# Value matmuls in four column tiles of 32, another order of the first pair, and half of the input weights decoded from round 18 on

## The chip, the cores and the metric

The kernel runs on one core of a Trainium2 chip. The core has a matrix engine (TensorE, PE in the rows; its weight loads are PEld), a vector engine (VectorE, DVE), a scalar engine (ScalarE, ACT), GpSimd (POOL) and SyncE (SP), which issues most DMAs. Each engine runs its own list of instructions in order and waits on semaphores for the others. The metric is device time in microseconds, the median of several runs.

## What is computed

Three layers, one after the other, for 2 batches, 12 heads, 448 positions, head size 64:

```python
# attention with a soft cap
scores = cap * tanh(q @ k.T / sqrt(64) / cap)
attn = exp(scores - max) ; attn = attn / (sum(attn) + 1e-9)
x = attn @ v                                  # heads side by side: 448 x 768
# gated MLP with a spatial gate
u, v = split(gelu(x @ w_in))                  # w_in 768 x 1024
x = x + (u * (w_sg @ layernorm(v) + b_sg)) @ w_out
# gated MLP with a convolution of 3 positions
h = relu(x @ w2_in)                           # 768 x 1024
out = (h * sigmoid(conv(h))) @ w2_out         # 1024 x 768
```

## The kernel before

Attention comes first, in 12 pairs of heads (N), each in two halves; a half is a round R = 2N + half, and two more rounds follow. All matmuls of attention go through `ordered`, which pins each behind the one before it, so TensorE's order is the order of the code. A round has these parts:

- `scores(N, half)` (line 308) writes keys times queries into the tile `sc`, four banks, one buffer. Keys stand in four blocks g of 128. For g = 0 to 2 each head has its own matmuls, on its half of the partitions, two at a time; g = 3 holds the last 64 keys of one head and the first 64 of the other in one matmul. Half 0 has g = 0 and 1 (12 matmuls), half 1 has g = 2 and 3 (9). ScalarE then does tanh (line 317, out of `sc` into `raw`) and exp (line 318, in `raw`). For pair 0 tanh and exp go block by block. The next scores need the banks that tanh has read.
- `values(N, half)` (line 344) runs a round later, from round 13 on two. It multiplies `raw` with the values into the tile `pv` (lines 353 to 361: two matmuls of 64 columns for each g below 3, one of 128 columns for g = 3, in float32, each of which the profile shows as two instructions), and then sums `raw` over the keys into `su` (lines 363 to 372) in four column tiles of 32, on half 0 by way of `sm`, in which VectorE has added two blocks (line 342). `su` has one buffer, which VectorE copies into `se` (line 389); ScalarE copies `pv` into `E` (line 390).
- `norm` sends the sums through DMAs (`ss`, `d`, `rb`), VectorE multiplies and splits into `X`. The last pair goes through TensorE instead (`norm_pe`, line 431, tiles `r` and `rp`; `rp` lies in the bank of `su`).
- `prep_q` and `prep_k` split a later pair's queries and keys on VectorE.
- A piece of the input weights w_in (12 pieces of 128 rows and 512 columns, 0 to 5 into `WI0`, 6 to 11 into `WI1`) is loaded by SP in the round that the table `WIN` names, `int(at * 4 + 1) // 2`, and decoded from 64-bit words some ticks later (`decode`, line 121; two ticks a round): ScalarE line 130, VectorE lines 135, 140, 143, 149 and 152, tile `f`. Before: rounds 0, 2, 4, 5, 7, 9, 11, 13, 14, 16, 18, 20.
- In the rounds of the table `FILL` (13, 17, 21: 6 matmuls; 23, 25: 18 matmuls) TensorE also does parts of x @ w_in with `WI0` (tile `mo`).

Ahead of it all, `WARM` matmuls of zeros run while the first loads are under way, and `IDLE` matmuls of zeros (tile `idle`) run behind the first two blocks of pair 0. In round 1, `values(0, 0)` runs between the scores of g = 2 and g = 3.

The eight banks of PSUM: one for `mo` in the pool psm, seven in the pool psa (`sc` four, `pv` two, `su` one) in the order in which the tags first ask. After attention a pool `ps1` of seven banks takes their place in the same order, and its first user is the first unit at line 603 (`v_unit`, X times `WI1`); it must wait for the last reader of its bank. From there on TensorE goes unit by unit through the two MLPs. VectorE, ScalarE and SP lists are put into order by the scheduler.

Of the kernel before, what the change touches and what calls it, by code (L numbers as in the profile page):

```python
# [9 lines left out]
F32 = mybir.dt.float32  # L10
# [6 lines left out]
P = 128  # L17
B, H, S, D = 2, 12, 448, 64
# [16 lines left out]

TAKEN = 3

WARM = 10

IDLE = 5  # L40

WIN = tuple(0.9 * j for j in range(12))
WOS = (0, 1, 4, 7, 7, 10, 11, 15)
W2I = (12, 12, 13, 13, 15, 17, 22, 24, 26, 30, 30, 33)
W2O = (0, 0, 1, 3, 4, 6, 7, 8, 8, 10, 10, 11, 11, 11, 11, 12, 13, 14, 15, 17, 18, 18, 19, 19)
# [3 lines left out]
def stages(  # L49
# [169 lines left out]
    def attention(att, psa):  # L219
# [26 lines left out]
        vf = {}  # L246
# [29 lines left out]
        load_v(0)  # L276
        if WARM:

            wz = att.tile([P, S], F32R, name="wz")
            V.memset(f(wz), 0.0)  # L280
            wps = psa.tile([P, 512], F32, tag="su", name="wps", bufs=1)[:, :S]
            for i in range(WARM):
                T.matmul(wps, lhsT=wz[:, :P], rhs=wz, start=True, stop=True)
        constants(att)
# [17 lines left out]
        def ordered(*args, **kw):  # L302

            with pin(lastm):
                lastm[0] = T.matmul(*args, **kw)  # L305


        def scores(N, half, between=None):

            q, K = Qt[N], Kt[N % 2]  # L310
            ps = psa.tile([P, 4, 512], F32, tag="sc", name="sc", bufs=1)
# [6 lines left out]
                lasta[0] = A.activation(raw[:, t], raw[:, t], AF.Exp, scale=capc)  # L318

            for g in range(2 * half, 2 * half + 2):  # L320
                c = slice(g * P, (g + 1) * P)
                t = g % 2 * 2
                if g < 3:

                    for i, (j, l) in enumerate(((0, 0), (0, 1), (1, 0))):
                        for h in range(2):
                            r = slice(h * D, (h + 1) * D)
                            ordered(ps[:, t + h, :S], lhsT=K[r, j, c], rhs=q[r, l], start=i == 0, stop=i == 2)
                else:

                    mm3(ps[:, t, :S], K[:, 0, c], K[:, 1, c], q[:, 0], q[:, 1], True, True, ordered)
                if N == 0:
                    soft(slice(t, t + (2 if g < 3 else 1)))
                    for _ in range(IDLE if g < 2 else 0):
                        ordered(idle, lhsT=wz[:, :P], rhs=wz, start=True, stop=True)
                if between and g == 2:
                    between()
            if N:
                soft(slice(0, 4 - half))
            if half == 0:  # L340
                held[N] = att.tile([P, 2, S], F32, tag="sm", name="sm", bufs=2)
                V.tensor_tensor(out=held[N], in0=raw[:, 0:2], in1=raw[:, 2:4], op=ALU.add)

        def values(N, half):
            if half == 0:
                acc[N] = (
                    psa.tile([P, 512], F32, tag="pv", name="pv", bufs=2)[:, :S],
                    psa.tile([P, 512], F32, tag="su", name="su", bufs=1)[:, : S // 2],
                )
            ps, su = acc[N]  # L350
            raw = raws.pop((N, half))
            for g in range(2 * half, 2 * half + 2):
                if g < 3:
                    for h in range(2):
                        r = slice(h * D, (h + 1) * D)
                        ordered(
                            ps[r], lhsT=vf[N][:, g, r], rhs=raw[:, g % 2 * 2 + h],
                            start=g == 0, stop=False, skip_group_check=True,
                        )
                else:  # L360
                    ordered(ps, lhsT=vf[N][:, 3], rhs=raw[:, 2], start=False, stop=True, skip_group_check=True)

            for g in range(2 * half, 3 * half + 1):
                x = raw if half else held.pop(N)
# [86 lines left out]
        done = 0  # L451
        for R in range(2 * NN + LAGS[1]):
# [6 lines left out]
            if R < 2 * NN:  # L459
                if half == 0 and N + 2 < NN:  # L460
                    load(N + 2)
                if R == 1:

                    scores(N, half, lambda: values(0, 0))
                    done += 1
                else:
                    scores(N, half)
                if half == 0 and N + 1 < NN:
                    prep_q(N + 1)
                    prep_k(N + 1)  # L470
# [427 lines left out]
```

## Time and profile before

| | |
|---|---|
| median of 3 runs | 342.35 us (340.76, 342.35, 344.26) |
| the profiled execution | 343.89 us, span 342.1 us |
| TensorE busy | 329.2 us (96%) |
| VectorE busy | 252.9 us (74%) |
| ScalarE busy | 224.9 us (66%) |
| GpSimd busy | 35.8 us (10%) |

Shares are of the span. Times within the program are counted from the start of the span. A row of the order of time gives start, duration, engine, line, operation and tiles, with the idle time before it and what ended it in brackets. The ends of matmuls are modelled; the distance between two starts is the better measure.

### The profile page before, as it was taken

How to read it: one execution, taken by the hardware profiler on the slowest of the kernel's cores; microseconds unless marked ns; L12 is line 12 of the kernel's file. 1: busy time of each engine (PE TensorE's matmuls, PEld its weight loads, DVE VectorE, ACT ScalarE, POOL GpSimd, SP SyncE). 2: the span in 40 equal slices, each digit the busy share in tenths (PEclk: the TensorE clock that was granted, in tenths of full speed). 3: DMA queues.
4: the chain of work that ended last, by engine and by line, in shares of the span. 5: the costliest groups of instructions: out<-in, count | busy, mean ns of one | idle time of the engine just before them, and what ended most of it. 6: DMA issues, size and time to landing. Idle time of an engine off the chain costs nothing.

```text
span 342.1 us, 5132 instructions
## 1 busy us (share of the span) xinstructions
PE 329.2 (96%) x1814; PEld 252.2 (74%) x1814; DVE 252.9 (74%) x493; ACT 224.9 (66%) x361; POOL 35.8 (10%) x71
## 2 busy tenths in 40 slices
PE   5999999999999999999999999999999999999992
PEld 4544444544456558898899999999999999999991
DVE  3378878889974477997999779997995999970000
ACT  1689988997897246576875554465884988873110
POOL 3000300311034113121111000000000000000000
PEclk9699999999999999999999999999999999999998
DMA  5859555748122114313123383002284113013111
GB/s 174 243 143 278 178 156 158 216 118 218 47 66 63 44 54 148 93 46 94 62 68 119 107 281 150 0 0 62 63 273 158 33 61 92 3 55 126 64 55 34
DMA packets 18698, 37.67 MB, mean 110 GB/s; under 512 B 3980, under 2 KB 9160, under 8 KB 18664
## 3 DMA queue, kind: packets, MB, share of 16 engines
q1 hardware_dynamic: 16952, 34.41, 32.7%
q0 software_dynamic: 1472, 2.61, 2.9%
q8 instruction: 16, 0.26, 0.4%
q10 hardware_dynamic: 240, 0.23, 0.2%
q14 instruction: 18, 0.15, 0.1%
HBM read 34.41 MB, written 2.79 MB: 109 GB/s over the span
## 4 chain that ended last, share of the span: by engine, by line
PE 79%; DMA 7%; DVE 7%; issue 3%; POOL 1%; ACT 0%; SPq 0%; DVEq 0%; ACTq 0%; POOLq 0%
PE mo L98 18%; PE mo L99 17%; PE mo L100 17%; PE pv L305 6%; PE sc L305 5%; PE mo L603 3%; PE mo L604 3%; PE mo L605 3%; PE mo L305 3%; PE su L305 3%; DMA kr<-in_kT_dram 2%; DMA ss<-se 2%; DMA qr<-in_qT_dram 2%; PE idle L305 1%; DVE Q L263 1%
## 5 line engine op out<-in xcount | busy, mean ns | idle before, releaser
L98 PE MATMUL mo<-X,WI 128*128 128x448 f32 x126 | 46.1, 367 | 0.0
L99 PE MATMUL mo<-X,WI 128*128 128x448 f32 x126 | 45.9, 366 | 0.0
L100 PE MATMUL mo<-X,WI 128*128 128x448 f32 x126 | 45.9, 365 | 0.0
L305 PE MATMUL pv<-raw,V 128*64 128x448 f32 (+1 forms) x168 | 43.7, 561 | 0.0
L305 PE MATMUL sc<-Q,K 64*128 64x448 f32 (+1 forms) x252 | 39.7, 398 | 3.4 <-DVE K L92 2.3
L318 ACT ACTIVATE raw<-raw,one 128x1792 f32<-128x1792 f32 (+3 forms) x26 | 39.1, 1503 | 0.6
L305 PEld LDWEIGHTS sc<-Q,K 64*128 64x128 f32 (+1 forms) x252 | 24.8, 190 | 18.0 <-issue 8.1
L130 ACT ACTIVATE f<-f 128x512 f32<-128x512 f32 (+3 forms) x57 | 30.9, 544 | 10.4 <-DMA f<-in_w_out_dram 6.0
L140 DVE SCALAR_TENSOR_TENSOR f<-f 128x512 uint32<-128x512 uint32 (+3 forms) x57 | 30.7, 547 | 9.2 <-ACT f L133 8.7
L317 ACT ACTIVATE raw<-sc 128x1792 f32<-128x1792 f32 (+1 forms) x22 | 32.5, 1475 | 6.8 <-PE sc L305 5.9
L99 PE MATMUL mo<-HG,W 128*128 128x448 f32 x96 | 34.8, 365 | 0.0
L100 PE MATMUL mo<-HG,W 128*128 128x448 f32 x96 | 34.7, 365 | 0.0
L98 PE MATMUL mo<-HG,W 128*128 128x448 f32 x96 | 34.1, 365 | 0.0
L143 DVE SCALAR_TENSOR_TENSOR f<-f 128x512 uint32<-128x512 uint32 (+3 forms) x57 | 30.9, 548 | 0.2
L305 PEld LDWEIGHTS pv<-raw,V 128*64 128x64 f32 (+1 forms) x168 | 11.8, 143 | 21.4 <-issue 18.6
L98 PEld LDWEIGHTS mo<-X,WI 128*128 128x128 f32 x126 | 23.6, 188 | 2.4 <-DVE u L179 0.4
L99 PEld LDWEIGHTS mo<-X,WI 128*128 128x128 f32 x126 | 23.7, 188 | 2.0
L100 PEld LDWEIGHTS mo<-X,WI 128*128 128x128 f32 x126 | 23.6, 188 | 2.0
L783 ACT ACTIVATE o<-mo 128x448 f32<-128x448 f32 x12 | 6.3, 540 | 25.6 <-PE mo L100 22.5
L133 ACT ACTIVATE f<-f 128x256 uint32<-128x256 uint32 (+2 forms) x44 | 22.6, 514 | 0.0
L99 PEld LDWEIGHTS mo<-HG,W 128*128 128x128 f32 x96 | 18.0, 188 | 1.4
L98 PEld LDWEIGHTS mo<-HG,W 128*128 128x128 f32 x96 | 18.0, 188 | 1.4
(141 smaller groups left out, 653.3 us busy)
## 6 DMA issues: line engine op xcount, KB each, us to landing
f<-in_w_in_dram SPq DMA_DIRECT2D x24, 512.0 KB, 4.9
f<-in_w_out_dram SPq DMA_DIRECT2D x24, 256.0 KB, 4.4
V<-in_vL_dram SPq DMA_DIRECT2D x12, 256.0 KB, 4.2
f<-in_w_out_dram SPq DMA_DIRECT2D x8, 384.0 KB, 3.1
qr<-in_qT_dram SPq DMA_DIRECT2D x24, 112.0 KB, 3.2
out_dram<-o SPq DMA_DIRECT2D x12, 224.0 KB, 1.9
rb<-d POOLq DMA_DIRECT2D x22, 112.0 KB, 3.2
kr<-in_kT_dram SPq DMA_DIRECT2D x11, 112.0 KB, 2.6
```

The source lines that it names most:

```text
L98: matmul(ps, lhsT=whi, rhs=xhi, start=start, stop=False)
L99: matmul(ps, lhsT=whi, rhs=xlo, start=False, stop=False)
L100: matmul(ps, lhsT=wlo, rhs=xhi, start=False, stop=stop)
L130: A.activation(f(h), f(h), AF.Copy, scale=2.0**-112)
L133: A.activation(l, l, AF.Copy, scale=0.93 * 2.0**-29)
L140: V.scalar_tensor_tensor(out=l, in0=h, scalar=3, in1=l, op0=ALU.logical_shift_left, op1=ALU.bitwise_or)
L143: V.scalar_tensor_tensor(out=l, in0=h, scalar=0x80000000, in1=l, op0=ALU.bitwise_and, op1=ALU.bitwise_or)
L305: lastm[0] = T.matmul(*args, **kw)
L317: A.activation(raw[:, t], ps[:, t, :S], AF.Tanh, **sc)
L318: lasta[0] = A.activation(raw[:, t], raw[:, t], AF.Exp, scale=capc)
L603: T.matmul(ps, lhsT=xs(0, k), rhs=WI[1][:, 0, k], start=k == 0, stop=False)
L604: T.matmul(ps, lhsT=xs(0, k), rhs=WI[1][:, 1, k], start=False, stop=False)
```

## The change

Seven edits. The zeros of the warm-up go into a bank of the tag `sc` instead of `su`, so the scores' four banks are the first of the pool, and there are 18 of them instead of 10. Behind pair 0's first block four idle matmuls stay, behind its second none. `value` does a block of the values in four matmuls of 32 columns each, the last block too. In round 1 the values of block 0 go ahead of the scores of g = 2, those of block 1 ahead of g = 3, and the sums behind g = 3. `WIN` now names rounds 0, 3, 6, 9, 12, 15 for the first half of the weights and 18 to 23 for the second.

```diff
-WARM = 10
-IDLE = 5
-WIN = tuple(0.9 * j for j in range(12))
+WARM = 18
+IDLE = 4
+WIN = (0, 1.5, 3, 4.5, 6, 7.5, 9, 9.5, 10, 10.5, 11, 11.5)
@@
-            wps = psa.tile([P, 512], F32, tag="su", name="wps", bufs=1)[:, :S]
+            wps = psa.tile([P, 4, 512], F32, tag="sc", name="wps", bufs=1)[:, 0, :S]
@@
-        def scores(N, half, between=None):
+        def scores(N, half, ahead={}):
@@
             for g in range(2 * half, 2 * half + 2):
+                if g in ahead:
+                    ahead[g]()
@@
-                    for _ in range(IDLE if g < 2 else 0):
+                    for _ in range(IDLE if g == 0 else 0):
                         ordered(idle, lhsT=wz[:, :P], rhs=wz, start=True, stop=True)
-                if between and g == 2:
-                    between()
@@
-        def values(N, half):
-            if half == 0:
-                acc[N] = (
-                    psa.tile([P, 512], F32, tag="pv", name="pv", bufs=2)[:, :S],
-                    psa.tile([P, 512], F32, tag="su", name="su", bufs=1)[:, : S // 2],
+        def start_values(N):
+            acc[N] = (
+                psa.tile([P, 512], F32, tag="pv", name="pv", bufs=2)[:, :S],
+                psa.tile([P, 512], F32, tag="su", name="su", bufs=1)[:, : S // 2],
+            )
+
+        def value(N, g):
+            raw = raws[N, g // 2]
+            for t in range(4):
+                r = slice(t * 32, (t + 1) * 32)
+                ordered(
+                    acc[N][0][r], lhsT=vf[N][:, g, r], rhs=raw[:, g % 2 * 2 + t // 2 if g < 3 else 2],
+                    start=g == 0, stop=g == 3, tile_position=(0, t * 32), skip_group_check=True,
                 )
+
+        def values(N, half, done=False):
+            if not done:
+                if half == 0:
+                    start_values(N)
+                value(N, 2 * half)
+                value(N, 2 * half + 1)
             ps, su = acc[N]
             raw = raws.pop((N, half))
-            for g in range(2 * half, 2 * half + 2):
-                if g < 3:
-                    for h in range(2):
-                        r = slice(h * D, (h + 1) * D)
-                        ordered(
-                            ps[r], lhsT=vf[N][:, g, r], rhs=raw[:, g % 2 * 2 + h],
-                            start=g == 0, stop=False, skip_group_check=True,
-                        )
-                else:
-                    ordered(ps, lhsT=vf[N][:, 3], rhs=raw[:, 2], start=False, stop=True, skip_group_check=True)
@@
-                    scores(N, half, lambda: values(0, 0))
+                    start_values(0)
+                    scores(N, half, {2: lambda: value(0, 0), 3: lambda: value(0, 1)})
+                    values(0, 0, True)
```

What moves on TensorE at the start: the piece of the difference behind the first six scores, down to pair 1's first scores.

```order
-L305 MATMUL idle<-wz 128x448 x5
+L305 MATMUL idle<-wz 128x448 x4
 L305 MATMUL sc<-Q,K_87 128x448 x6
-L305 MATMUL idle<-wz 128x448 x5
+L305 MATMUL pv<-raw,V 32x448 x4
 L305 MATMUL sc<-Q,K_87 128x448 x6
-L305 MATMUL pv<-raw,V 64x448 x4
-L305 MATMUL su<-sm,ones_138 32x224 x4
+L305 MATMUL pv<-raw,V 32x448 x4
 L305 MATMUL sc<-Q,K_87 128x448 x3
+L305 MATMUL su<-sm,ones_146 32x224 x4
 L305 MATMUL sc<-Q,K_88 128x448 x12
```

Each half of the values stands ahead of a block of scores, and the sums, which need `sm`, stand behind the last (`ones` are columns of ones, K_87 and K_88 the key buffers of even and odd pairs).

On VectorE, late in attention: before, behind the last `sm` (line 342, pair 11) come a unit's two steps (lines 175 and 179, for `mo`), the product for `E` and the copy that frees `su`.

```order
L342 TENSOR_TENSOR sm<-raw 128x896
L175 SCALAR_TENSOR_TENSOR g_1134<-g_1134,mo 128x448
L179 SCALAR_TENSOR_TENSOR u<-g_1134,mo 128x448
L423 TENSOR_TENSOR E<-E,rb 128x896
L389 COPY se<-su 128x224
```

In the changed kernel the same place has a whole piece of the weights (`f_1084`) and the first step of another ahead of the same copy, now line 394.

```order
L342 TENSOR_TENSOR sm<-raw 128x896
L140 SCALAR_TENSOR_TENSOR f_1084<-f_1084 128x512
L143 SCALAR_TENSOR_TENSOR f_1084<-f_1084 128x512
L149 CAST WI_77<-f_1084 128x512
L152 TENSOR_TENSOR WI_77<-f_1084,WI_77 128x512
L175 SCALAR_TENSOR_TENSOR g_1214<-g_1214,mo 128x448
L179 SCALAR_TENSOR_TENSOR u<-g_1214,mo 128x448
L428 TENSOR_TENSOR E<-E,rb 128x896
L140 SCALAR_TENSOR_TENSOR f_1140<-f_1140 128x512
L394 COPY se<-su 128x224
```

The rest of `f_1140` and one more whole piece stand between this copy and the reciprocal that `rp` needs.

## Rows read from the trace of the kernel before

**Rows 1.** Stretches: length, busy us and instructions by engine, clock, DMA share, GB/s.

```profile
19.43:84.59 65.16, 64.01 (x468) 30.25 (x469) 55.15 (x107) 60.25 (x55) 11.09 (x18) 1.00 0.63 181
84.59:122.29 37.70, 37.58 (x262) 20.08 (x258) 24.96 (x45) 26.33 (x26) 9.72 (x16) 1.00 0.22 60
127.96:335.70 207.74, 207.74 (x1006) 188.73 (x1006) 160.28 (x317) 127.85 (x268) 11.86 (x15) 1.00 0.28 91
```

**Rows 2.** TensorE's waits: who waited for whom, us, times, longest.

```profile
PE sc L305 <- ACT raw L317: 1.0, 2, 0.7
PE mo L603 <- DVE E L446: 0.8, 1, 0.8
PE su L305 <- DVE se L389: 0.8, 1, 0.8
```

**Rows 3.** Order of time on TensorE, the start of attention.

```profile
1.38 3.86 PE L283 MATMUL wps<-wz 128*128 128x448 f32 x10 [1.38 <-DVE wz L280]
7.55 1.47 PE L305 MATMUL sc<-Q,K 64*128 64x448 f32 x6 [2.31 <-DVE K L92]
...
11.11 1.49 PE L305 MATMUL sc<-Q,K 64*128 64x448 f32 x6
...
17.31 0.58 PE L305 MATMUL su<-sm,ones 128*32 128x224 f32 x8
...
19.43 0.88 PE L305 MATMUL sc<-Q,K 64*128 64x448 f32 x6 [0.72 <-ACT raw L317]
```

**Rows 4.** Order of time on TensorE, one steady pair.

```profile
33.16 1.72 PE L305 MATMUL pv<-raw,V 128*64 128x448 f32 x8
34.81 0.59 PE L305 MATMUL su<-sm,ones 128*32 128x224 f32 x8
35.33 1.49 PE L305 MATMUL sc<-Q,K 64*128 64x448 f32 x12
36.74 1.92 PE L305 MATMUL pv<-raw,V 128*64 128x448 f32 x6
38.59 0.96 PE L305 MATMUL su<-raw,ones 128*32 128x224 f32 x16
39.49 1.68 PE L305 MATMUL sc<-Q,K 64*128 64x448 f32 x9
41.10 1.72 PE L305 MATMUL pv<-raw,V 128*64 128x448 f32 x8
```

**Rows 5.** Order of time on ScalarE and VectorE, pair 0.

```profile
9.07 1.01 ACT L317 ACTIVATE raw<-sc,one 128x896 f32<-128x896 f32 x1 [2.26 <-PE sc L305]
10.11 1.04 ACT L318 ACTIVATE raw<-raw,one 128x896 f32<-128x896 f32 x1
...
15.06 0.18 DVE L135 TENSOR_SCALAR f<-f 128x24 uint32<-128x24 uint32 x1 [4.34 <-DMA f<-in_conv_w_dram]
15.15 1.09 DVE L342 TENSOR_TENSOR sm<-raw 128x896 f32<-128x896 f32 x1
```

**Rows 6.** Stretches of the start, TensorE alone: length, busy, clock, DMA share, GB/s.

```profile
5.20:7.50 2.30, 0.04 (x1) 1.00 0.65 160
...
8.24:15.00 6.76, 6.72 (x20) 0.50 0.85 231
```

**Rows 7.** Stretches, tile f alone: length, VectorE, ScalarE, clock, DMA share, GB/s.

```profile
19.43:84.59 65.16, 26.08 (x48) 7.07 (x12) 1.00 0.63 181
84.59:122.29 37.70, 8.61 (x14) 1.34 (x2) 1.00 0.22 60
```

**Rows 8.** Order of time on TensorE, the wait for VectorE's copy.

```profile
78.49 0.59 PE L305 MATMUL su<-sm,ones 128*32 128x224 f32 x8 [0.83 <-DVE se L389]
```

**Rows 9.** Order of time on ScalarE, one steady pair.

```profile
36.85 1.67 ACT L317 ACTIVATE raw<-sc 128x1792 f32<-128x1792 f32 x1 [0.28 <-PE sc L305]
38.70 0.54 ACT L390 ACTIVATE E<-pv 128x448 f32<-128x448 f32 x1 [0.18 <-PE pv L305]
39.14 1.78 ACT L318 ACTIVATE raw<-raw,one 128x1792 f32<-128x1792 f32 x1
```

## Prediction

> **What bounds the kernel now.** I read the stretches first. From 127.96 us to 335.70 us TensorE is busy for 207.74 of 207.74 us [rows 1]: nothing there waits, so whatever time the matrix engine reaches the first gated-MLP unit at line 603 earlier is kept to the end. From 19.43 to 122.29 it is nearly the same, 64.01 of 65.16 and 37.58 of 37.70 us [rows 1]. The list of what TensorE waits for holds only three small things from 19 us on: 1.0 us for ScalarE's tanh in two places, 0.8 us for a VectorE copy that frees the `su` bank, and 0.8 us before line 603 for the VectorE product that still reads that bank [rows 2]. So attention is bound by TensorE, with ScalarE close behind: 60.25 of 65.16 us busy up to 84.59, VectorE 55.15 [rows 1]. The start is different: with one pair in flight, scores, tanh, exp and values wait for each other until 19.43 us, when the second pair's scores start [rows 3].
>
> **Values in 32 columns.** A steady pair is in [rows 4]. One half: eight `pv` instructions (four matmuls, each in two instructions) from 33.16 to 34.81, then eight `su` to 35.33. The other: six `pv` from 36.74 to 38.59, sixteen `su` to 39.49. Sixteen `su` take 0.90 and eight 0.52, so four more of them, one wave of four column tiles, take 0.19 and what is left, 0.14, is paid once per block. A wave streams 224 columns; 448 columns take twice that, 0.375. Eight `pv` of 64 columns are four waves of two, 1.50, and they measured 1.65: again 0.15 for the change of tile shape. Six `pv` are two waves of two and two full-width instructions, 1.50, and measured 1.85: two changes of shape. After the change `pv` is sixteen instructions in waves of four, 4 x 0.375 = 1.50, in the shape that `su` has, so the change of shape between them goes. Half 0: 1.50 + 0.52 = 2.02 instead of 2.17; half 1: 1.50 + 0.90 = 2.40 instead of 2.75. That is 0.50 a pair; for eleven pairs and the second half of pair 0, **-5.85 us**. The matrix work itself is not smaller; only the changes go. Bounds: the gain is 0 if each block pays its 0.15 somewhere else, and 12 x 0.50 = 6.0 at most.
>
> This hangs on four 448-column streams running abreast. [rows 4] show it for `su`: four 32-column tiles with four different 224-column inputs, 0.19 a wave, half of what two 64-column tiles with 448 columns take. The Trainium skill (TensorE: Matmul & The Clock Gate, Part 3, measured speedups) gives 2.38x for three 32-column tiles, not three. By that, as an estimate, a wave would take 0.375 x 3 / 2.38 = 0.47 and the sum would come to some 344.5 us; the `su` rows show no such loss, at half the length.
>
> **The start.** The changed order puts pair 0's value matmuls between its scores, and the sums behind the last scores. The ScalarE chain decides, tanh 1.01 and exp 1.04 for two banks [rows 5]. Today the first scores end at 9.02, five idle matmuls run, and the second scores come at 11.11; TensorE stands at half its clock through this, 0.50 from 8.24 to 15.00 after it had 0.04 us of work in 2.30 us from 5.20 on [rows 6]: that is the 1.2 GHz level, and 2.4 before and after. Ten warm-up matmuls end at 1.38 + 3.86 = 5.24 [rows 3]; eight more, 0.19 each at the upper level that stands from 5.20 on, reach to about 6.7 and leave 0.8 us of rest instead of 2.3, so I take the upper level for the scores. Then, by the rows: first scores done at 8.65 (9.02 less 2 x 0.19, for the passes that run below full clock today), tanh to 9.7, exp to 10.8; second scores after that tanh (their row waits for ScalarE) done by 10.5; tanh 11.8, exp 12.85; third scores need the bank that this tanh frees, tanh 13.9, exp 14.9; fourth scores after 13.9, tanh of one bank to 15.55. By that chain pair 1's scores could start at 15.6. But the sums wait for `sm`, and VectorE does `sm` behind the shift of the convolution weights, whose load lands at 15.06: `sm` 15.15 to 16.24 [rows 5]. Nothing in the change moves these two. The sums then start at 16.3, today 17.31, take 0.52, and pair 1's scores start at 16.85 instead of 19.43: **-2.6 us**. Bounds: at the lower clock throughout, the second scores (behind four idle matmuls instead of five) are done at 12.2, their tanh at 13.25, values and third scores at 15.4, tanh 16.5, fourth scores 17.2, and sums and last tanh at 18.2 (-1.2); if the weights land earlier because the second 512 KB load now stands behind pair 2's, up to 15.6 (-3.8).
>
> **The bank order.** Today the first unit at line 603 waits 0.8 us, for the product at line 446, which reads the bank of `su` [rows 2]. With the scores' four banks first in the pool, the unit's first bank is one that tanh left long ago: **-0.84 us**. It is hidden if something else is late there (below).
>
> **The decode.** A piece is five VectorE instructions: 26.08 us for 48 of them up to 84.59, 2.7 a piece, and 8.61 for 14 after it, 3.1 a piece; on ScalarE 0.6 [rows 7]. Up to 84.59 there are now 9.6 pieces' worth and there will be 6: VectorE falls from 55.15 by 9.8 to 45.4 us, in a stretch of some 61. The stall of 0.83 us for `su`'s copy stands in this stretch, at 78.49 [rows 8], behind a queue of decode work; it should go: **-0.83 us**. From 84.59 on there were 2.8 pieces and will be 6: 24.96 + 3.2 x 3.0 = 34.5 us in 37.70 - 2.0 = 35.7. That is 97% on an engine that takes its work in order and also waits there for DMA: it will trail. What stands behind the decode in VectorE's queue (the two pieces of its order above) is the copy `se` that frees `su`'s bank, and the reciprocal `r` for which `rp` waits. I expect each to be late once, together **+1.4 us** (one 0.9, one 0.5; bounds 0 and 4, a whole piece and a bit).
>
> **ScalarE's round.** From a pair's scores to the end of its first exp it is 39.14 + 1.78 - 35.33 = 5.59, of which 0.18 is a wait for `pv` that the shorter `pv` removes [rows 4, 9]. So 5.41 and a handover, against TensorE's 1.41 + 2.40 + 1.62 = 5.43 until it wants that exp. Equal: TensorE will wait about 0.1 a pair, and 0.2 to 0.5 in the rounds where a decode piece (0.6) falls between exp and tanh or TensorE has the sums behind it already. Taken together **+1.5 us** (bounds 0 and 3.5).
>
> **The sum.** -5.85 - 2.6 - 0.84 - 0.83 + 1.4 + 1.5 = -7.2 us. The profiled execution took 343.89 us (span 342.1), which gives 336.7; it is the slow end of the three timed runs (340.76 to 344.26), so against the median of 342.35 I say **335.2 us**, 2.1% less. A measurement of this kernel can tell about 1% from no change.
>
> **Rivals.**
> *The softmax ring and VectorE give it back.* ScalarE waits at their upper bound and VectorE 4 us late: -10.1 + 3.5 + 4 = -2.6, 339.7 us. For it: 92% on ScalarE today, 97% on VectorE after. Against it: TensorE waits for ScalarE only twice now, and the decode that moves into rounds 18 to 23 meets rounds in which TensorE has fill work for it to hide behind (18 `mo` matmuls in each of two of them). 18 in 100.
> *The clock is not held at the start.* The longer warm-up ends, TensorE rests, and with six fewer idle matmuls the lower level lasts longer than today: -1.2 instead of -2.6, and half a further pair's 7.45 us at half clock, +3.7. Sum -2.1, 340.2 us. This is the case in which a part of the change does not do what it says. For it: today ten idle matmuls and the level still fell. 10 in 100.
> *Slower: the four tiles hinder each other at 448 columns.* If every wave of four pays what a change of shape costs a block, 0.15, the 24 halves with 4 waves each take +14.4, and the sum is 349.6 us; if they go two by two, each half takes 3.0 instead of 1.50 and the sum is 371. It decides from a wave of 0.485 on: 24 x 4 x 0.11 = +10.6 turns -7.2 into slower by 1%. Against it stand the `su` rows, four abreast at full pace. 5 in 100.
> *The same, but milder.* At two thirds of that, 0.10 a wave, it is 24 x 4 x 0.10 = +9.6, 344.8 us, no change. 4 in 100, for the same reason. About there the ratio of the Trainium skill named above (TensorE: Matmul & The Clock Gate, Part 3) would put it.
> *More than I count.* ScalarE and VectorE keep up and the weights land early: -5.85 - 3.8 - 0.84 - 0.83 = -11.3, 331 us. 8 in 100.
> My own case, 333 to 338, has 55 in 100.
>
> **How the numbers follow.** The range 331.5 to 340.5 takes in my case, the two rivals that give part back, and most of the better one, and leaves out about 18 in 100. Faster by over 1% means under 338.9: my case, the better one, and about half of the two that give part back, 55 + 8 + 14 = 77 in 100. Within 1%: the other half of these and the milder loss, 18 in 100. Slower: 5 in 100.
>
> **What would show it.** Right: a pair in about 7.45 us where it took 7.95; `pv` sixteen instructions in 1.50 with `su` right behind; pair 1's scores at about 16.9 us; line 603 reached at about 121 us; no wait for the product behind `rp`; TensorE without a gap after that. Wrong: `pv` over 1.7 us; a granted clock of 0.50 past 15 us; waits of TensorE for tanh or exp above 3 us in sum; `su` or `rp` waiting for VectorE behind 90 us for more than 4 us; a gap in TensorE behind line 603, if VectorE carries its lateness over.

## The result and the profile after

The changed kernel takes **337.56 us** in the median of four executions (336.00 to 339.26), the kernel before 342.00 (340.76 to 344.26, four executions); the ratio is 0.9875, 95% interval 0.9836 to 0.9915. So it is faster by 1.25%; the interval goes from 0.85% to 1.64%, so it is clear of no change, and a gain over 1% is likely but not certain. It is slower than the 335.2 us forecast. The profiled execution took 336.94 us, its span 335.2 us.

The stretches of the changed kernel (columns as in [rows 1]) begin where pair 1's scores begin:

```profile
16.80:78.00 61.20, 60.97 (x614) 31.29 (x612) 47.57 (x91) 56.38 (x48) 11.30 (x18) 1.00 0.65 182
78.00:115.31 37.31, 35.10 (x327) 19.82 (x323) 31.74 (x60) 28.18 (x30) 9.16 (x15) 1.00 0.31 96
115.31:121.30 5.99, 4.99 (x31) 3.91 (x28) 5.52 (x8) 1.74 (x3) 0.59 (x2) 1.00 0.28 77
121.30:329.00 207.70, 207.67 (x1006) 188.82 (x1006) 160.17 (x317) 127.77 (x268) 11.86 (x15) 1.00 0.28 91
```

Behind 121.30 us TensorE is again busy all the time, 207.67 of 207.70 us. Everything that changed lies ahead of the first unit of the gated MLP, which is line 610 now (603 before).

TensorE's waits, as in [rows 2]:

```profile
PE su L305 <- DVE se L394: 1.8, 1, 1.8
PE su L305 <- DVE sm L342: 1.6, 1, 1.6
...
PE mo L610 <- DVE E L451: 0.8, 1, 0.8
PE sc L305 <- ACT raw L317: 0.6, 2, 0.4
```

Two of [rows 2] are still there under new line numbers: `mo` for the product that reads `rp` (0.8) and `sc` for tanh (0.6). The wait for the copy of the sums grew from 0.8 to 1.8. New is `su` waiting 1.6 for `sm`.

The start in order of time on TensorE, which answers to [rows 3], and its clock, which answers to [rows 6]:

```profile
1.38 5.32 PE L283 MATMUL wps<-wz 128*128 128x448 f32 x18 [1.38 <-DVE wz L280]
7.61 1.11 PE L305 MATMUL sc<-Q,K 64*128 64x448 f32 x6 [0.91 <-DVE K L92]
...
16.29 0.59 PE L305 MATMUL su<-sm,ones 128*32 128x224 f32 x8 [1.62 <-DVE sm L342]
16.80 0.88 PE L305 MATMUL sc<-Q,K 64*128 64x448 f32 x6
```

```profile
8.24:15.00 6.76, 5.93 (x39) 1.00 0.81 235
```

Pair 1's scores start at 16.80 instead of 19.43 us, and the granted clock is 1.00 where it was 0.50.

A steady pair, which answers to [rows 4]:

```profile
33.19 1.71 PE L305 MATMUL pv<-raw,V 128*32 128x448 f32 x16
34.72 0.94 PE L305 MATMUL su<-raw,ones 128*32 128x224 f32 x16
35.59 1.69 PE L305 MATMUL sc<-Q,K 64*128 64x448 f32 x9
37.25 1.71 PE L305 MATMUL pv<-raw,V 128*32 128x448 f32 x16
38.78 0.56 PE L305 MATMUL su<-sm,ones 128*32 128x224 f32 x8
39.27 1.49 PE L305 MATMUL sc<-Q,K 64*128 64x448 f32 x12
40.69 1.71 PE L305 MATMUL pv<-raw,V 128*32 128x448 f32 x16
```

Sixteen `pv` take 1.53 us from start to start in either half; half 0 takes 39.27 - 37.25 = 2.02, half 1 35.59 - 33.19 = 2.40, and the pair 40.69 - 33.19 = 7.50 instead of 7.95.

### The profile page after: what moved, and what is told of

It reads as the page before. It is cut to its first block, busy times and chain, and to the rows that moved or that the text cites. A ratio compares the mean times of both kernels' runs of the same rounds, so it can differ in the third digit from the quotient of the medians.

```text
span 335.2 us, 5571 instructions
## 1 busy us (share of the span) xinstructions
PE 321.1 (96%) x2032; PEld 251.5 (75%) x2032; DVE 252.3 (75%) x493; ACT 223.9 (67%) x361; POOL 36.1 (11%) x71
## 4 chain that ended last, share of the span: by engine, by line
PE 63%; issue 16%; DMA 8%; POOL 4%; DVE 4%; SPq 3%; ACT 0%; POOLq 0%; DVEq 0%; ACTq 0%
PE mo L98 18%; PE mo L99 18%; PE mo L100 18%; DMA d<-ss 3%; POOL rb L421 3%; PE mo L610 3%; PE mo L611 3%; PE mo L612 3%; DMA qr<-in_qT_dram 2%; DMA kr<-in_kT_dram 2%; SPq L238 1%; POOL ss L402 1%; DMA ss<-se 1%; DVE K L95 1%; PE mo L657 0%
## 5 line engine op out<-in xcount | busy, mean ns | idle before, releaser
L305 PE MATMUL pv<-raw,V 128*32 128x448 f32 x384 | 41.2, 545 | 0.4 <-ACT raw L318 0.4
L305 PE MATMUL sc<-Q,K 64*128 64x448 f32 (+1 forms) x252 | 38.7, 389 | 1.6 <-DVE K L92 0.9
L305 PEld LDWEIGHTS pv<-raw,V 128*32 128x32 f32 x384 | 10.0, 109 | 19.5 <-issue 15.6
L342 DVE TENSOR_TENSOR sm<-raw 128x896 f32<-128x896 f32 x12 | 13.0, 1086 | 9.6 <-ACT raw L318 9.6
L99 PEld LDWEIGHTS mo<-HG,W 128*128 128x128 f32 x96 | 18.1, 188 | 1.4
```

Source lines behind the costliest of these rows:

```text
L99: matmul(ps, lhsT=whi, rhs=xlo, start=False, stop=False)
```

## Two marks for every kernel

All kernels here have the same tail: from the first matmul of that MLP unit to the end of the span it is 214.0 to 214.3 us in every trace. So two marks on TensorE are enough to compare them: S, where pair 1's scores start, and U, where the unit's first matmul starts. The table has them for each trace, with the medians and the ratio to the kernel before, timed beside each.

| kernel | S | U | U - S | median us | ratio (95%) |
|---|---|---|---|---|---|
| before | 19.43 | 127.96 | 108.53 | 342.00 | |
| before, second trace | 18.11 | 125.69 | 107.58 | 341.71 (one) | |
| changed | 16.80 | 121.21 | 104.41 | 337.56 | 0.9875 (0.9836, 0.9915) |
| before + values in 32 | 18.15 | 123.53 | 105.38 | 339.17 | 0.9905 (0.9873, 0.9938) |
| changed, old values | 16.98 | 127.22 | 110.24 | 340.77 | 0.9954 (0.9928, 0.9979) |
| changed, values in 64 | 16.83 | 124.31 | 107.48 | 339.55 | 0.9909 (0.9878, 0.9940) |
| changed, old decode table | 17.08 | 121.45 | 104.37 | 337.90 | 0.9874 (0.9832, 0.9915) |
| changed, waits by tile | 16.72 | 119.63 | 102.91 | 338.04 | 0.9882 (0.9841, 0.9923) |
| the same, `su` bank first | 16.81 | 120.36 | 103.55 | 336.48 (one) | |
| changed, 10 warm-up matmuls | 17.41 | 124.58 | 107.17 | 338.80 | 0.9896 (0.9863, 0.9930) |
| changed, late conv weights | 15.37 | 119.44 | 104.07 | 335.43 | 0.9785 (0.9746, 0.9824) |
| waits by tile, filled wait | 16.89 | 122.64 | 105.75 | 338.57 | 0.9883 (0.9844, 0.9922) |
| late weights, waits by tile | 15.38 | 120.96 | 105.58 | 334.71 | 0.9754 (0.9708, 0.9800) |
| the same, spread decode | 15.28 | 118.89 | 103.61 | 334.86 | 0.9752 (0.9709, 0.9796) |

A trace is one execution; the medians are over 4 to 10 (the kernel before 4 to 23). The traced execution is not always a typical one: of "changed, old values" (343.32 us) and of "late weights, waits by tile" (336.93) it is the slowest, of "changed, waits by tile" (335.62) the fastest. So U is compared here only together with the waits that a trace shows.

## Experiments: the values

**The values alone**, in the kernel before:

```diff
-                if g < 3:
-                    for h in range(2):
-                        r = slice(h * D, (h + 1) * D)
-                        ordered(ps[r], ..., rhs=raw[:, g % 2 * 2 + h], ...)
-                else:
-                    ordered(ps, lhsT=vf[N][:, 3], rhs=raw[:, 2], ...)
+                for t in range(4):
+                    r = slice(t * 32, (t + 1) * 32)
+                    ordered(ps[r], ..., rhs=raw[:, g % 2 * 2 + t // 2 if g < 3 else 2],
+                            ..., tile_position=(0, t * 32), ...)
```

> The kernel before, with nothing changed but the value matmuls, which go in four column tiles of 32 (all blocks, also the last). Bank order, warm-up, order of pair 0 and the table of the decode stay. Theory of the prediction (a price per change of tile shape, 0.15 a block of instructions): half 0's values 1.50 to 1.53 us with the sums right behind, half 1 the same, a steady pair 7.45 to 7.50 us instead of 7.95, so about 5.9 less, of which the softmax ring and VectorE, which still has 9.6 decode pieces in a stretch that is now 5 us shorter, give back 1 to 2: 337.5 to 339 us against a kernel before of 342, line 603's first matmul 4 to 5 us earlier than 127.96. Rival A (the price is paid elsewhere, at the scores): pairs of 7.8 to 7.95, no gain. Rival B (VectorE cannot follow without the moved decode): pairs as in the theory, but waits for the copy of the sums of 3 us or more in sum, 340 us or more.

It is 339.17 us, 3.1 less than the 342.3 beside it, just above the expected 337.5 to 339. A steady pair takes 7.50. Waits for VectorE appear, 1.5 us for the copy of the sums in two places and 0.5 for `sm`: less than rival B's 3 us, but with tanh and the end of attention 3.9 us of waits stand between S and U, where the second trace of the kernel before has 1.2. The unit comes at 123.53, 4.4 us earlier than in the first trace of the kernel before, but 1.3 of that is the start, which is not changed here (S 18.15 and 19.43). So the term of the values is real, and waits eat about half of it here.

**The old values** in the changed kernel (the same diff turned round).

> The changed kernel with the value matmuls as they were (two of 64 columns a block, one of 128 for the last block); start, bank order and decode table stay changed. Theory: the steady pair is back at 7.95 and the kernel gives up nearly all of 5.9 us, less what it no longer waits for ScalarE and for the copy of the sums (1.0 and 1.8 in the changed kernel): 4 to 5.5 above the changed kernel, 341.5 to 343 us, no more than 1 us from the kernel before in the median; what is left is the start, pair 1's scores at about 17.0. Rival: the start alone is worth its full 2.6 in every execution, and the kernel is 2 to 3 us faster than the kernel before.

340.77 us, a little under the expected 341.5 to 343, 3.2 above the changed kernel and 1.5 under the kernel before (the rival had 2 to 3). That it gives up no more is in part that waits go: between S and U they sum to 2.1 us, in the changed kernel to 3.4. The pair is back at 7.95 (26.50, 34.44, 42.39 are starts of successive scores). The first pair after S takes 26.50 - 16.98 = 9.52, and the profile tells why (TensorE alone; length, busy, clock, DMA share, GB/s):

```profile
14.50:16.40 1.90, 0.23 (x2) 1.00 0.91 219
...
18.00:21.00 3.00, 3.00 (x11) 0.50 0.97 299
22.00:26.00 4.00, 4.00 (x36) 1.00 0.93 283
```

TensorE rests 1.73 us for `sm`, until 16.46, and from about 17.9 to 21.3 it runs at 0.50, the 1.2 GHz level: 9.52 - 7.95 = 1.57 us lost.

**Two tiles of 64 for every block**, to price one change of shape.

```diff
-            for t in range(4):
-                r = slice(t * 32, (t + 1) * 32)
+            for h in range(2):
+                r = slice(h * D, (h + 1) * D)
```

> The changed kernel with the values in two column tiles of 64 for all four blocks, the last one too (it went in one tile of 128 columns before). Theory (0.15 us for each change of tile shape, none for the width): half 0 as before the change, 1.65 for the values and 0.52 for the sums, 2.17; half 1 has one change left of two, 1.65 and 0.90, 2.55 instead of 2.75; a steady pair at 7.49 + 0.15 + 0.15 = 7.79 us, so 11.5 pairs cost 3.4 us more than the changed kernel, less up to 1 us of waits that go: 340 to 341. Rival (only the block of 128 columns costs; four tiles of 32 bring nothing over two of 64): a steady pair at 7.5 and no difference.

339.55 us, just under the expected 340 to 341, and a steady pair of 41.64 - 33.89 = 7.75 us (7.79 expected):

```profile
33.89 1.49 PE L305 MATMUL sc<-Q,K 64*128 64x448 f32 x12
35.31 1.72 PE L305 MATMUL pv<-raw,V 128*64 128x448 f32 x8
36.96 0.96 PE L305 MATMUL su<-raw,ones 128*32 128x224 f32 x16
37.86 1.68 PE L305 MATMUL sc<-Q,K 64*128 64x448 f32 x9
39.47 1.72 PE L305 MATMUL pv<-raw,V 128*64 128x448 f32 x8
41.12 0.59 PE L305 MATMUL su<-sm,ones 128*32 128x224 f32 x8
41.64 1.49 PE L305 MATMUL sc<-Q,K 64*128 64x448 f32 x12
```

Eight `pv` of 64 columns take 1.65 in both halves, sixteen of 32 columns 1.53, for the same streamed columns. The last block's full-width matmul cost more on top: pairs of 7.95 (64 and 128 columns), 7.75 (64) and 7.50 (32). The rival, that only the full-width block costs, is out. That it is the change of shape that costs and not the wider tile is seen at the start, where one block stands alone between scores, so that either width meets a change on both sides. With tiles of 64 and, in the changed kernel, of 32:

```profile
10.86 0.97 PE L305 MATMUL pv<-raw,V 128*64 128x448 f32 x4 [0.19 <-ACT raw L318]
11.77 0.88 PE L305 MATMUL sc<-Q,K 64*128 64x448 f32 x6
```

```profile
10.90 0.96 PE L305 MATMUL pv<-raw,V 128*32 128x448 f32 x8 [0.20 <-ACT raw L318]
11.81 0.88 PE L305 MATMUL sc<-Q,K 64*128 64x448 f32 x6
```

A block takes 0.91 us in both. Only next to the sums, whose shape the tiles of 32 share, do the widths differ, by 0.12 in the values and 0.03 in the sums behind them (0.87 and 0.49 instead of 0.90 and 0.52).

## Experiments: the decode

**The old table** in the changed kernel.

```diff
-WIN = (0, 1.5, 3, 4.5, 6, 7.5, 9, 9.5, 10, 10.5, 11, 11.5)
+WIN = tuple(0.9 * j for j in range(12))
```

> The changed kernel with the old table of the decode (a piece every 1.8 rounds, the last in round 20). The prediction's step says that moving the decode wins a stall of 0.83 near 78 us and costs 1.4 behind 85 us; the changed kernel's trace shows 1.80 there. By that, undoing it takes the 1.80 away and puts 0.8 to 1.0 back before 85 us: 0.5 to 1.0 us faster than the changed kernel, line 610 at 120.2 to 120.7 instead of 121.21. Rival: with pairs of 7.5 instead of 7.95 the old table loads VectorE by 9.6 pieces in 60 us and the stalls before 85 us grow to 2 to 4 us: 1 to 2 us slower than the changed kernel, line 610 at 122 to 123.

337.90 us, and U - S is 104.37 against 104.41: no difference, neither the gain of 0.5 to 1.0 nor the rival's loss. The wait of 1.80 for the copy goes, and waits for ScalarE come: 0.56 for an exp, 0.71, 0.53 and 0.39 for tanh, where the changed kernel has 0.17 and 0.41. Ahead of the three late tanh ScalarE's share of a decode piece, some 0.6 us (line 130, at 60.66, 71.54 and 88.22), stands between an exp and the next tanh. Moving the decode moved the waits, and their sum between S and U is nearly the same, 3.2 and 3.4.

Where the 1.80 comes from, VectorE in the changed kernel in order of time:

```profile
95.79 0.38 DVE L394 COPY se<-su 128x224 f32<-128x224 f32 x1
...
100.81 0.23 DVE L411 TENSOR_SCALAR ss<-ss,one 128x14 f32<-128x14 f32 x1 [2.08 <-DMA ss<-se]
...
101.23 1.03 DVE L342 TENSOR_TENSOR sm<-raw 128x896 f32<-128x896 f32 x1
102.18 0.68 DVE L140 SCALAR_TENSOR_TENSOR f<-f 128x512 uint32<-128x512 uint32 x1
...
107.49 0.68 DVE L140 SCALAR_TENSOR_TENSOR f<-f 128x512 uint32<-128x512 uint32 x1
108.09 0.38 DVE L394 COPY se<-su 128x224 f32<-128x224 f32 x1
```

The copy of the sums at 95.79 goes out by DMA, which takes 4.3 us from its issue, and is back only at 100.8; VectorE stands at line 411 for 2.08 us with `sm` and a whole decode piece queued behind, and the next copy comes at 108.09. VectorE is not full here (31.74 of 37.31 us), but its list has little to spare between these two points: in the seven traces with this table and values of 32 columns, VectorE's wait for this DMA is 1.24 to 2.48 us and the next copy is late by that less 0.28 to 0.31.

The DMA's time goes with the table. At this place (the fifth of six such DMAs) it takes 3.4 to 4.7 us in the nine traces with the changed table and 2.2 to 2.5 in the five with another; the DMA engines are busy 47 to 78% in the 3.5 us behind its issue in the nine, 10 to 17% in the five. The pieces of weights that are still being loaded may slow it, but no run shows that alone, and elsewhere in these traces the same DMA took 3.6 us at 9% and 2.4 at 47%; the reason stays open. The wait that the prediction took for decode work, 0.83 at 78.49 [rows 8], also has a late DMA of sums ahead of it, in the kernel before:

```profile
69.74 0.23 DVE L406 TENSOR_SCALAR ss<-ss,one 128x14 f32<-128x14 f32 x1 [1.95 <-DMA ss<-se]
```

That DMA took 5.1 us. In the second trace of that kernel (below) it took 3.3, VectorE has no wait at this line, and TensorE none for the copy.

## Experiments: the banks

**Waits by tile** for the pool that follows attention.

```diff
-tc.tile_pool(name="ps1", bufs=7, space=PSUM)
+tc.tile_pool(name="ps1", bufs=7, space=PSUM, reuse_waits="tile")
```

> The changed kernel with the pool of the banks after attention set to wait tile by tile for what lay in its place, not for the whole pool of attention. Theory (new): the bank order of the change does nothing, because the new pool waits for the last reader of the whole old pool, the product at line 451, whichever bank comes first. With waits by tile the first unit's bank is one of the scores, free since the last tanh, and the wait of 0.84 goes: line 610's first matmul right behind the last of line 447, at about 120.4 instead of 121.21, 0.8 us less to the end. Rival: the first unit waits for the split of the last pair's X (line 94 or 95), not for a bank; then the start stays at 121.2 and nothing changes.

The wait of 0.84 goes. Ahead of the unit the changed kernel has

```profile
119.39 0.98 PE L447 MATMUL rp<-r,sel 128*64 128x224 f32 x8
121.21 0.47 PE L610 MATMUL mo<-WI,X 128*128 128x512 f32 x1 [0.84 <-DVE E L451]
```

and the kernel with waits by tile

```profile
118.73 0.98 PE L447 MATMUL rp<-r,sel 128*64 128x224 f32 x8
119.63 0.50 PE L610 MATMUL mo<-WI,X 128*128 128x512 f32 x1
```

1.82 us from `rp` to the unit against 0.90. (U is lower by 1.58; 0.74 of it is that in this execution the copy of the sums was 1.06 late instead of 1.80.) The median, 338.04 over executions from 335.62 to 338.94, is too wide to show 0.9 us.

**The bank of the sums first** again, still with waits by tile.

```diff
-wps = psa.tile([P, 4, 512], F32, tag="sc", name="wps", bufs=1)[:, 0, :S]
+wps = psa.tile([P, 512], F32, tag="su", name="wps", bufs=1)[:, :S]
```

> The changed kernel with the pool behind attention waiting tile by tile, as in the run that took the wait of 0.84 away, and with the zeros of the warm-up in the bank of the sums again, so that this bank comes first. Theory: the first unit's bank is now that of rp, and the wait for the product at line 451 is back: line 610 begins 0.8 us behind the last matmul of line 447. So the order of the banks matters only where waits go by tile. Rival: with waits by tile the order does not matter either, and line 610's first matmul begins ahead of or right behind line 447's last.

```profile
120.36 0.50 PE L610 MATMUL mo<-WI,X 128*128 128x512 f32 x1 [0.75 <-DVE E L451]
```

The wait is back, 0.75 us. So a new pool waits for the last reader of the whole pool that lay there, whichever bank comes first; only with waits by tile does the last reader of its own bank count, and only then does the order decide. (The description of the kernel before says its own bank for the pool as it was; that is not so.) The bank order of the change alone brings nothing.

## Experiments: the start

**A second trace of the kernel before.**

> The kernel before, unchanged, for a second trace of its start. The prediction priced the start against one execution (343.89 us, pair 1's scores at 19.43, a stretch of 6.8 us at a granted clock of 0.50). Theory: that execution was a late one; the kernel with only the values changed has the same start and began pair 1's scores at 18.15, with 3.4 us at 0.50. So in this trace pair 1's scores start between 17.9 and 18.7 us, the first matmul of line 603 follows 108.3 to 108.8 us behind them as before, and the span is 340.0 to 341.3. Rival: the start is 19.2 to 19.6 in nearly every execution, and what the profiled sum of 7.2 us lacks in the medians lies elsewhere, behind pair 1's scores.

S is 18.11, as the theory had it, and U - S 107.58, 0.7 under the expected bound (the span, 339.8 us, is 0.2 under its own): the wait of 0.83 for the copy of the sums [rows 8] isn't in this execution. U comes at 125.69, 2.27 us ahead of the trace on which the prediction was worked out, and U of the changed kernel 4.48 ahead of that. The medians differ by 4.44.

Its first rows show what the granted clock does not:

```profile
8.52 2.23 PE L305 MATMUL idle<-wz 128*128 128x448 f32 x5
10.68 0.88 PE L305 MATMUL sc<-Q,K 64*128 64x448 f32 x6
11.49 1.29 PE L305 MATMUL idle<-wz 128*128 128x448 f32 x5
12.71 0.88 PE L305 MATMUL sc<-Q,K 64*128 64x448 f32 x6
```

```profile
8.50:11.00 2.50, 2.50 (x11) 1.00 0.84 271
```

Five idle matmuls take 10.68 - 8.52 = 2.16 us, then 1.22, though the clock is recorded as 1.00 throughout; in the first trace both groups took 2.16, with 0.50 on record.

**Ten warm-up matmuls** in the changed kernel (WARM = 10).

> The changed kernel with 10 warm-up matmuls instead of 18; four idle matmuls and all else stay. Theory: without the longer warm-up TensorE rests some 2 us ahead of pair 0's scores, and a stretch at a granted clock of 0.50 (1.2 GHz) stands behind it, as in both profiles of kernels with the old warm-up: there it was 3.4 us long (8.6 to 12.1) in one and 6.8 us (8.2 to 15.1) in the other. The first scores then take 1.5 us instead of 1.1, but the sums of pair 0 wait for VectorE's sm behind the convolution weights until 16.2 to 16.5 either way. So with the short stretch pair 1's scores start at 16.8 to 17.2, no later than now, with the long one at 17.5 to 18.2: 0 to 1.5 us more than the changed kernel, 337.5 to 339. Rival (prediction's second rival at its full price): the lower level lasts past 16 us, half a pair more at half clock, +3 to +4, 341 us.

338.80 us, in the expected 337.5 to 339; S is 17.41, between the two expected ranges (16.8 to 17.2, 17.5 to 18.2). In the trace the clock is 0.50 from about 8.2 to 11.7 us, where the changed kernel's is 1.00: the longer warm-up does what it was priced for. But `sm` still holds the sums, here until 16.89, after a wait of 1.38; S is 0.6 later than in the changed kernel because the convolution weights land 0.6 later (VectorE's shift of them at 15.57 instead of 14.97). So the lower level cost nothing at S that the load had not cost already; the medians, 1.2 us apart, have intervals that overlap.

**The convolution weights late**, in round 6, and with them the gain of the layer norm, which `columns` loads just ahead of them.

```diff
-            if R == 1:
+            if R == 6:
                 columns(att)
```

> The changed kernel with the loads of the convolution weights and of the gain of the layer norm issued in round 6 instead of round 1. Theory: VectorE's 4.3 us of waiting for these weights is what holds back sm, and sm holds back the sums and pair 1's scores; without it the sums follow pair 0's last scores at once, and pair 1's scores wait for the last tanh only: 15.2 to 15.6 us instead of 16.8. TensorE then has no wait of 1.6 us at 14.7, behind which one of the profiles so far showed a stretch of 3.4 us at a granted clock of 0.50, so that stretch goes too from executions that have it: 1.2 to 1.6 us less than the changed kernel in every execution, up to 3 in some, 334.5 to 336.3 in the median. Rival: the loads of pairs 1 and 2, not the convolution weights, decide (the key splits of pair 2 stand right behind sm on VectorE), and pair 1's scores stay at 16.5 to 17, no gain.

335.43 us (334.50 to 336.88), as the theory had it. VectorE does `sm` at 12.84, as soon as exp is done, and TensorE does not wait for it:

```profile
14.58 0.58 PE L305 MATMUL su<-sm,ones 128*32 128x224 f32 x8
15.37 1.49 PE L305 MATMUL sc<-Q,K 64*128 64x448 f32 x12 [0.21 <-ACT raw L317]
```

S is 15.37, 1.43 under the changed kernel. A load of 24 KB held the start, whose first use for the convolution comes at 230 us; 256 KB for the gain, first used at 137 us, are issued ahead of it. Which of the two loads makes it late is not tested.

**The wait filled** with zeros, in the kernel with waits by tile.

```diff
                     scores(N, half, {2: lambda: value(0, 0), 3: lambda: value(0, 1)})
+                    for _ in range(8):
+                        ordered(idle, lhsT=wz[:, :P], rhs=wz, start=True, stop=True)
                     values(0, 0, True)
```

> The kernel with waits by tile (its runs 335.62 to 338.94, with mean clocks of 0.998 down to 0.992), and eight matmuls of zeros, 0.19 each, between pair 0's last scores and its sums, where TensorE waits 1.8 us for sm. The wait stays, the sums start at 16.2 to 16.4 as before; TensorE only isn't idle in it. Theory: behind this wait a stretch of 3.4 us at a granted clock of 0.50 stands in some executions (two of the traces so far show it there, 1.6 us each), and that is a good part of the spread between executions. So with the matmuls in it no execution has that stretch: the fastest stays at 335.6 to 336.2, the slow ones of 338 to 339 become rare, the median comes to 336.0 to 337.0. Rival: the spread comes from when the loads land, or from the later wait for the copy of the sums, and runs and clocks scatter as before, median 337.5 to 338.2.

338.57 us (338.00 to 340.46): the theory's 336 to 337 is missed, and the run decides nothing. The added matmuls also changed the scheduler's order, and new waits stand elsewhere:

```profile
21.41 1.69 PE L305 MATMUL sc<-Q,K 64*128 64x448 f32 x9 [0.64 <-ACT raw L317]
23.52 1.71 PE L305 MATMUL pv<-raw,V 128*32 128x448 f32 x16 [0.42 <-ACT raw L318]
...
117.88 0.47 PE L98 MATMUL mo<-X,WI 128*128 128x448 f32 x1 [1.55 <-DVE u L179]
```

Together 2.6 us, of which the changed kernel has 0.16. The first two stand behind a new order on ScalarE: a step of the convolution weights (line 147) that waits 2.92 us for VectorE now stands ahead of pair 1's first tanh. The third is no matter of order: VectorE's list there is the same, but it stands 1.70 us for the DMA of the last sums (0.28 in the kernel with waits by tile). Whether the fill alone keeps the clock up stays open.

## Experiments: a faster version

**Late weights and waits by tile** together.

> The changed kernel with the convolution weights loaded in round 6 and the pool behind attention waiting tile by tile, the two edits that each ran alone. Theory: they lie at different places, so they add: pair 1's scores at 15.2 to 15.5, line 610's first unit begun before rp's product is done, 1.4 + 1.0 to 1.6 us less than the changed kernel, 334 to 335 us in the median, 2.2 to 2.5 per cent under the kernel before. Rival: the earlier unit only moves TensorE's wait behind it (the units behind it need the last X splits, or the gelu of an earlier unit), and the time is that of the late load alone, 335.4.

334.71 us in the median, inside the expected range, though too close to the late load alone (335.43) to show the second edit by the medians. The traced execution took 336.93: the copy of the sums is 2.01 us late at 107.6, and behind that rest the clock falls (length, busy, clock, DMA share, GB/s):

```profile
109.20:112.40 3.20, 3.20 (x10) 0.51 0.10 7
113.00:118.00 5.00, 4.84 (x45) 1.00 0.28 83
```

From that `su` to the first matmul of line 98 it takes 116.17 - 107.62 = 8.55 us, in the changed kernel 115.54 - 108.53 = 7.01: 1.54 us lost behind a rest of 2.01.

**The decode spread otherwise** on top of it.

```diff
-WIN = (0, 1.5, 3, 4.5, 6, 7.5, 9, 9.5, 10, 10.5, 11, 11.5)
+WIN = (0, 1, 2, 5, 5.5, 7.5, 6, 7, 9, 9.5, 11, 11.5)
```

> As the kernel with both edits, and the decode's pieces spread otherwise: rounds 0, 2, 4, 10, 11, 15 for the first half of the weights and 12, 14, 18, 19, 22, 23 for the second, so that three pieces instead of four stand on VectorE between rounds 18 and 22, ahead of the copy of the sums that came 1.0 to 1.8 us late at 107 us. Theory (VectorE's order there makes that wait): it goes, small ones of 0.3 come at 71 and 87 us, 0.5 to 1.0 us less than with both edits alone, 333.3 to 334.3. Rival (the sum of waits stays what it is, as with the old table, whose waits lay elsewhere and cost the same): no difference, within 0.3 us.

334.86 us, the median of the kernel above: the rival. The copy of the sums is 0.56 late instead of 1 to 2 us, and waits for tanh stand in its place: behind S 1.7 us (0.94, 0.39 and 0.39), where the kernel above has 0.55. VectorE's wait for the DMA is longer, but the decode pieces between the two copies are gone but for one step, and the DMA itself takes 2.5 us:

```profile
98.46 0.23 DVE L411 TENSOR_SCALAR ss<-ss,one 128x14 f32<-128x14 f32 x1 [2.78 <-DMA ss<-se]
...
106.68 0.38 DVE L394 COPY se<-su 128x224 f32<-128x224 f32 x1
```

What differs is the spread: six executions between 334.55 and 335.03. Both versions beat the changed kernel, by 0.8% (334.71 and 334.86 against 337.56) or by 1.2% if each is taken by its ratio to the kernel before, whose intervals do not overlap, and the kernel before by 2.5%.

## Why the prediction came out as it did

The sum was -7.2 us from the profiled 343.89, to 336.7; the profiled execution of the changed kernel took 336.94. Term by term, between these two traces:

- **Values, -5.85: right, a little large.** Halves of 2.02 and 2.40, as worked out. The pair is 7.50 rather than 7.45 because 0.06 of the 0.50 is paid again at the scores: the nine take 37.25 - 35.59 = 1.66 where they took 1.61 [rows 4], the twelve 1.42 instead of 1.41. That is a small piece of the prediction's lower bound, by which each block pays its price somewhere else. So the term is, as an estimate, 11 x 0.45 + 0.35 = 5.3. The mechanism is shown by the kernels with 64 columns and with the old values. A wave of four tiles measured 1.53 / 4 = 0.38, so the tiles do not hinder each other here. The Trainium skill's ratio for three column tiles (TensorE: Matmul & The Clock Gate, Part 3, measured speedups) would have made a wave 0.47, as an estimate; four show no such loss here. That a change of tiling mode drains the array stands in the Trainium skill (TensorEngine Tiling (Array Packing), Tiling Modes, Key Properties) without a price. Here a half with tiles of 64 took 0.15 us longer than one with tiles of 32.
- **Start, -2.6: right against that trace**, 19.43 to 16.80, and through the step named: the sums wait for `sm`, and `sm` for the convolution weights. But 19.43 was the start of a late execution (below).
- **Bank order, -0.84: wrong.** "The unit's first bank is one that tanh left long ago" took the wait to be on a bank. It is on the pool, as the two kernels with waits by tile show.
- **Decode, -0.83 and +1.4: right in sign, for a part of the reason.** The copy of the sums is late once, 1.80, and `r` is not late at all. Behind 78 us VectorE is busy 31.74 of 37.31 us, 85% and not 97%; the copy is late because a DMA came back late and the list behind it, with the decode in it, had only 0.3 us to spare. The 0.83 stood behind a late DMA as well, in one of two executions. (The 48 instructions read as 9.6 pieces are nine pieces and three small ones of the convolution weights.) And the sum of the two terms does not hang on the table: with the old one the waits between S and U sum to nearly the same.
- **ScalarE's round, +1.5: too large.** Waits for ScalarE behind S are 0.17 and 0.41, against 0.32 before.

The last three points sum to +1.23 in the forecast (-0.84 - 0.83 + 1.4 + 1.5). Measured waits between S and U grew from 0.32 + 0.83 + 0.84 = 1.99 to 0.17 + 0.41 + 1.80 + 0.16 + 0.84 = 3.38, by 1.4. That the two agree is luck: the wait at the bank that stayed and the ones that were priced too high offset each other. Of the signs given, U came at 121.21 (about 121 forecast) and TensorE has no gap behind it; the wait behind `rp` is the one that did not go.

**The step that failed** is the last one, "so against the median of 342.35 I say 335.2". It took the whole 7.2 off the median, though part of it was the lateness of one execution of the kernel before: the long stretch at half pace (S at 19.43 instead of 18.11) and the late copy of the sums [rows 8]. In the second trace neither stands (its stretch at half pace is shorter, see its first rows), and from there the change is worth 18.11 - 16.80 = 1.31 at the start and 107.58 - 104.41 = 3.17 behind it, 4.48 in all. By the medians the parts agree: the values alone bring 3.1, all the rest without them 1.5, together 4.6; the change 4.4. So the start was mis-sized, 1.3 for 2.6, and the 0.83 of the decode was there to win in one execution of two.

**Of the rivals**, the clock at the start came true in some executions only: in two of six traces with the changed start and an unfilled wait for `sm` (old values, values in 64) it fell behind that wait, for 1.57 us and 1.56 (26.14 - 16.83 - 7.75). That is less than the rival's 3.7. How much of the spread of the changed kernel's executions it makes is not settled. The softmax ring and VectorE gave back less than the first rival's 3.5 and 4: 0.6 and 1.8 to 2.0 us of waits. Four tiles that hinder each other are out, with a wave of 0.38 against the 0.485 from which that rival would decide.

## What to carry to other kernels

Groups of matmuls that stand next to each other should have one tile shape; here it was worth more than half the instructions (1.53 us for sixteen, 1.65 for eight). A small load that is needed late does not belong ahead of the first work in an in-order queue, and it pays to ask whether a wait is for a tile or for a whole pool before reordering tiles. A gain worked out against one execution holds for that execution: compare a second trace of the kernel before, at the same marks, before taking it off a median.

## What was not expected of the hardware

A rest of TensorE may cost more than its own length, but not in every execution: a granted clock of 0.50 stood behind rests of 1.73, 1.69 and 2.01 us in three traces, 1.57, 1.56 and 1.54 us lost each, and none behind rests of 1.53, 1.62, 1.82 and 2.30 us for the same `sm`, nor behind 1.50, 1.80 and 2.17 us for the copy of the sums, in others. That the rest is the cause is argued, not shown: the run that filled one decided nothing. The kernel whose TensorE waits at most 0.94 us behind its first pair is also the one whose executions agree to 0.5 us (six of them), where the changed kernel's spread is 3.3 (four). And the recorded clock is not the whole pace: five matmuls of zeros took 2.16 us at a recorded 1.00 and the next five, in the same trace, 1.22, with nothing they waited for.
